# Attention into a soft mixture of experts: value tiles in one 128-row transfer, keys asked for earlier, key maxima and side work moved

## The chip, the cores and the metric

The kernel runs on one core of a Trainium2 chip. The metric is the device time of one execution in microseconds. Five engines matter, each with its own queue of instructions that it works off in order: PE (TensorE, matmuls and transposes; its weight loads are shown apart as PEld), DVE (VectorE), ACT (ScalarE), POOL (GpSimd) and SP (SyncE), which here only issues transfers from main memory. Semaphores order them between engines.

## The reference, cut to what matters

```python
# attention: q, k, v are (4 batches, 8 heads, 768 positions, 64), float32
k_sum = k.reshape(B, H, 24, 32, D).max(axis=3)      # one key per block of 32: the maximum
v_sum = v.reshape(B, H, 24, 32, D).mean(axis=3)     # and one value: the mean
scores_l = scale * q @ k.T, masked to |i - j| < 16  # the window
scores_s = scale * q @ k_sum.T + log(32)            # the 24 block keys
a = softmax(concat([scores_l, scores_s]))
x = a @ concat([v, v_sum])                          # -> (3072 tokens, 512)

# soft mixture of experts on x
logits = x @ phi                                    # (3072, 32 slots)
d = softmax of logits over the tokens;  slot_input = d.T @ x
slot_out[e] = relu(slot_input[e] @ w1[e]) @ w2[e]   # 8 experts, 4 slots each
c = softmax of logits over the slots;   return c @ slot_out
```

All of it is float32.

## The kernel before, in words

**Attention in 24 steps.** A step is 256 query positions of four heads. Three steps belong to one half of a batch's heads (`hb`, eight of them), which share one key tile; the table `STEPS` says which step is which, and `FIRST` = steps 0, 3, 6, 9, 12, 15, 18, 20 are those in which a new key tile is used for the first time. I call the step before each of these a boundary step (2, 5, 8, 11, 14, 17, 19).

In step `i` PE computes the scores of step `i` (`scores`, L210, into a PSUM tile `s` of which there is one), transposes the probabilities of step `j = i - 1` (`trans`, L253), and multiplies them with the values of step `j` (`values`, L268). DVE takes masked scores out of PSUM with their row minimum (`soft_max`, L231) and divides the previous step's output (`norm`, L283 to L285). ACT takes the exponentials (L240, L248) and moves the transposes out of PSUM (`evac`, L259). POOL subtracts the row values for the second half (`shift`, L244).

**Block keys.** The key tile holds, for each window of 64 keys, 24 columns kept free for the block maxima. `k_max` (L149, L158, L159, on DVE) reduces the tile, once for each of its two halves, and `k_put` (L164, POOL) copies the 24 maxima into each of the 12 windows, four windows first and then eight. `scores` of a `FIRST` step cannot start before its `k_put`.

**Block values.** A value tile `v` has 120 rows in use: 64 of the values, then 24 for block means, then 32 of the values. `v_sum` ("V" in the plans, L173) sums the values of three steps on PE; it needs all three value tiles of its half. `v_sel` ("S", L187) picks the 24 means, ACT copies them to `vsst`, and `put_v` (L196, POOL) copies them into rows 64 to 87 of each value tile.

**Side work.** The tables `PLAN_A` and `PLAN_B` place pieces of the second part between the steps: A between the transposes and `values`, B after `values`. X (or x) transposes 128 tokens of the attention's output and copies them out, on ACT for X and on DVE for x; L forms the logits of 512 tokens and, when the generator is run on, their maximum and exponentials; T transposes these, D multiplies them with the tokens and adds to `acc`. What a step started and did not finish stands in `pending` and is finished at the start of the next step.

**Transfers.** All are issued from SP, in the order of the program, at the end of each step: a key tile three steps before its use (`load_k`, two buffers), a query tile every other step (`load_q`, two buffers), the values of step `i + 5` (`load_v`, six buffers) and, by the table `LOADS`, pieces of expert weights of 512 KB (`load_piece`). The first 25 pieces have buffers of their own; the later ones take over buffers that attention has finished with. A transfer whose buffer is still in use holds up SP, and with it all that is behind it. `load_v` issues two transfers, one for 64 rows and one for 32.

**After attention** the rest of the routing follows, then a stream through the first expert matrices (L604), the second (L639) and the combination (L673), with the remaining weights loaded as buffers come free.

Of the kernel before, what the change touches and what calls it, by code (L numbers as in the profile page):

```python
# [18 lines left out]
NB = S // 32  # L19
HB = 2 * B  # L20
TPS = 3
NSTEP = HB * TPS
NQ = NT // 512
NW = S // 64

WA, WB = 64, 32
U = WA + NB + WB
SEG = WA + NB
KROW = SEG * (NW - 1) + U
VROW = 1152  # L30
NEG = -1.0e30
EPS = 1e-9

# [8 lines left out]
FIRST = [STEPS.index((hb, 0)) for hb in range(HB)]  # L42
STEP_OF = {s: i for i, s in enumerate(STEPS)}


LOADS = [0, 0, 1, 1, 1, 2, 1, 2, 1, 2, 1, 2, 1, 2, 1, 2, 1, 2, 2, 1, 1, 3, 2, 3]
NWA, NV, NX, NXT = 25, 6, 5, 4
LATE = "v v v k k v q p v q v p k r x x".split()


PLAN_A = {
    0: "V0", 3: "V1", 5: "X0", 6: "V2", 7: "X3", 8: "T0 X4", 9: "V3", 10: "X5", 11: "X6", 12: "V4", 13: "X8", 14: "X10",
    15: "V5", 16: "L2", 17: "X12", 18: "V6", 19: "X14", 20: "V7", 21: "X16", 22: "X18", 23: "L4", 24: "X20 T4",
}
PLAN_B = {
    0: "S0", 3: "S1", 5: "x1", 6: "S2 x2", 7: "L0", 9: "S3 D0", 11: "x7", 12: "S4 L1", 13: "x9 T1", 14: "D1",
    15: "S5 x11", 17: "x13 T2", 18: "S6 D2", 19: "x15", 20: "S7 L3", 21: "x17 T3", 22: "x19 D3", 24: "X21 D4",
}


# [1 line left out]
def attention_soft_moe(ctx: ExitStack, tc, kx, qx, vx, phi, wx, cst, out):  # L62

    nc = tc.nc
# [27 lines left out]
    wt = {}  # L92
# [25 lines left out]
    def load_k(hb, parts=1):  # L118
        if hb < HB:
            kt[hb] = kp.tile([128, 2, KROW], F32, name=f"k{hb}", tag="k")  # L120
            if parts == 1:
                nc.sync.dma_start(out=kt[hb].rearrange("p q k -> p (q k)"), in_=kx[hb].rearrange("p q k -> p (q k)"))
            else:
                for pr in range(2):
                    nc.sync.dma_start(out=kt[hb][:, pr], in_=kx[hb, :, pr])

    def load_q(n):
        if 2 * n < NSTEP:
            q = mx.tile([128, 2, 2, 256], F32, name=f"q{n}", tag="q")
            nc.sync.dma_start(out=q.rearrange("p i q t -> p (i q t)"), in_=qx[n])  # L130
            qt[2 * n], qt[2 * n + 1] = q[:, 0], q[:, 1]

    def load_v(i):
        if i < NSTEP:
            v = vp.tile([128, VROW], F32, name=f"v{i}", tag="v")
            nc.sync.dma_start(out=v[0:WA], in_=vx[i, 0:WA])
            nc.sync.dma_start(out=v[WA + NB : U], in_=vx[i, WA:])
            vt[i] = v[0:U, 0 : 16 * 65].rearrange("p (w h c) -> p w h c", w=4, h=4)


# [2 lines left out]
    def k_max(hb, pr):  # L143
        if pr == 0:
            ks[hb] = (
                wk.tile([128, 2, 4 * NW + 1], F32, name="k16", bufs=1), wk.tile([128, 2, NB], F32, name="ks", bufs=1)
            )
        k16, kb = ks[hb]
        nc.vector.reduce_max(  # L149
            out=k16[:, pr, 0 : 4 * NW].rearrange("p (w j) -> p w j", w=NW),  # L150
            in_=kt[hb][:, pr, 0 : SEG * NW].rearrange("p (w k) -> p w k", w=NW)[:, :, 0:WA].rearrange(
                "p w (j k) -> p w j k", j=4
            ),
            axis=AX,
        )
        if pr == 1:

            nc.vector.tensor_copy(out=k16[:, :, 4 * NW : 4 * NW + 1], in_=k16[:, :, 0:1])  # L158
            nc.vector.tensor_tensor(out=kb, in0=k16[:, :, 1 : 4 * NW : 2], in1=k16[:, :, 2 : 4 * NW + 1 : 2], op=ALU.max)  # L159

    def k_put(hb, eng, part=slice(0, NW)):
        dst = kt[hb][:, :, 0 : SEG * NW].rearrange("p q (w k) -> p q w k", w=NW)[:, :, part, WA:SEG]
        n = part.stop - part.start
        eng.tensor_copy(out=dst, in_=ks[hb][1].unsqueeze(2).broadcast_to([128, 2, n, NB]))  # L164
# [29 lines left out]
    def put_v(i, eng):  # L194
        src = vsst[STEPS[i][0] % 2][64 : 64 + NB].rearrange("n h c -> n (h c)").unsqueeze(1).broadcast_to([NB, 4, 260])
        eng.tensor_copy(out=vt[i][WA : WA + NB].rearrange("n w h c -> n w (h c)"), in_=src)  # L196
# [45 lines left out]
    def shift(i, r):  # L242
        p = p_[i][:, :, r]
        nc.gpsimd.tensor_tensor(out=p, in0=p, in1=m_[i, r].unsqueeze(2).broadcast_to([128, 4, U]), op=ALU.subtract)  # L244
# [11 lines left out]
    def evac(j, r):  # L256
        if r == 0:
            ptr_[j] = mx.tile([128, 2, 4, 128], F32, name="ptr", tag="r", bufs=1)
        nc.scalar.copy(out=ptr_[j][0:U, r], in_=ptr_[j, r])  # L259
# [188 lines left out]
    def flush(g):  # L448
        while advance(g):
            pass  # L450
# [9 lines left out]
    for i in range(TPS):  # L460
        load_v(i)
# [17 lines left out]
    def start(names):  # L479
        made = []  # L480
        for n in names.split():
            k, a = n[0], int(n[1:])
            if k in one_phase:
                one_phase[k](a)
            else:
                g = phased[k](a)
                advance(g)
                made.append(g)
                if k in "XxT":
                    flush(g)  # L490
                    made.pop()
        return made


    pending = []
    for i in range(NSTEP + 1):
        j = i - 1
        if i < NSTEP:
            scores(i)
        for g in pending:  # L500
            flush(g)
        if j in FIRST:
            put_v(j, nc.gpsimd)
        if j >= 0:
            trans(j, 0)
            trans(j, 1)
            evac(j, 0)
            evac(j, 1)
        if i < NSTEP:
            soft_max(i, 0)  # L510
            exp_units(i, 0)
            soft_max(i, 1)
            shift(i, 1)
            if i not in FIRST:
                put_v(i, nc.gpsimd)
        pending = start(PLAN_A.get(i, ""))
        if i < NSTEP:
            exp_wide(i, 1)
        if j >= 0:
            values(j, 0)  # L520
            values(j, 1)
        pending += start(PLAN_B.get(i, ""))
        if i + 1 in FIRST:
            hb = FIRST.index(i + 1)
            k_max(hb, 1)
            k_put(hb, nc.gpsimd, slice(0, 4))
            k_put(hb, nc.gpsimd, slice(4, NW))
        if j >= 0:
            norm(j)
        if i + 2 in FIRST:  # L530
            k_max(FIRST.index(i + 2), 0)
        if i < NSTEP:
            if i + 3 in FIRST[2:]:
                load_k(FIRST.index(i + 3))
            if i % 2:
                load_q((i + 3) // 2)
            load_v(i + 5)
            for _ in range(LOADS[i]):
                load_piece()

    tail.append(1)
# [58 lines left out]
    for k in range(32):  # L600
        e, c = divmod(k, 4)
# [21 lines left out]
    for i in range(2):  # L623
        nc.vector.tensor_copy(  # L624
            out=W2ST[i].rearrange("p j (e k) -> p j e k", e=NE)[:, :, :, 0:4],
            in_=ph[:, 128 * i : 128 * i + 128].rearrange("p (j e k) -> p j e k", j=4, e=NE),
# [85 lines left out]
def _layout(q, k, v, w1, w2):  # L712
    heads = np.arange(8).reshape(2, 2, 2)
    t = np.arange(NW)[:, None] * 64 - 16 + np.arange(64)[None, :]
    kx = np.zeros((HB, 128, 2, KROW), np.float32)
    qx = np.zeros((NSTEP // 2, 128, 2, 2, 256), np.float32)
    vx = np.ones((NSTEP, WA + WB, VROW), np.float32)
    for hb in range(HB):
        b, half = divmod(hb, 2)
        for pr in range(2):  # L720
            for r in range(2):
                h = heads[half, pr, r]
                kt = k[b, h].T
                rows = kx[hb, 64 * r : 64 * r + 64, pr]
                for w in range(NW):
                    rows[:, SEG * w : SEG * w + WA] = kt[:, t[w] % S]
                rows[:, SEG * NW :] = kt[:, np.arange(752, 784) % S]
                for tp in range(TPS):
                    n, i = divmod(STEP_OF[hb, tp], 2)
                    qx[n, 64 * r : 64 * r + 64, i, pr] = q[b, h, 256 * tp : 256 * tp + 256].T  # L730
        for w in range(NW):
            i, wi = STEP_OF[hb, w // 4], w % 4
            rows = (64 * w - 16 + np.arange(WA + WB)) % S

            for n in range(4):
                c = 65 * (4 * wi + n)
                vx[i, :, c : c + 64] = v[b, 4 * half + n, rows]
    wx = np.zeros((NPIECE, 128, 1024), np.float32)
    wx[0:32] = w1.reshape(NE * 4, 128, DF)
    n = 32  # L740

    wr = w2.reshape(NE, 4, 2, 128, DM)
    for c0, cn in CHUNKS:
        part = wr[..., c0 : c0 + cn].transpose(0, 2, 3, 1, 4)
        if cn == 128:
            part = part.transpose(0, 2, 1, 3, 4)
        part = part.reshape(-1, 128, 1024)
        wx[n : n + len(part)] = part
        n += len(part)
    return kx, qx.reshape(NSTEP // 2, 128, 1024), vx, wx  # L750
# [46 lines left out]
```

## Time and profile before

| what | value |
|---|---|
| three runs | 230.48, 233.22, 235.27 us; median 233.22 |
| the profiled execution | 228.62 us, of which the span of instructions is 226.7 |
| PE busy | 188.0 us, 83% |
| DVE, ACT, POOL busy | 125.6, 99.9, 58.4 us |
| moved by transfers | 66.54 MB, 293 GB/s on average |
| the queue that SP issues to | 90.5% of 16 transfer engines |

The span falls into a start until about 16 us, the steps 1 to 23 until about 158 us, the rest of the routing until about 171 us, and the expert stages. The table's shares are means over these. "PE busy" says nothing of the clock that PE ran at, which the profile lists apart.

### The profile page before, as it was taken

To read this page: it belongs to the slowest core of one execution; us is meant where nothing else is said; L and a number is where in the kernel's file an instruction comes from. 1 tells how busy PE (TensorE), PEld (TensorE's weight loads), DVE (VectorE), ACT (ScalarE), POOL (GpSimd) and SP (SyncE) were. 2 spreads that over 40 slices of the span, in tenths; PEclk is the share of its full clock that TensorE was granted. 3 is DMA by queue.
4 is the path that set the end of the run, shared out by engine and by line. 5 is a ranking of instruction groups with operands and counts; after the bars stand their busy time and mean duration, and the time that the engine had idled before them with its cause. 6 is when DMAs were issued, how large, how long until landed. Compare 5 with 4: busy or idle time off the path is not lost.

```text
span 226.7 us, 7484 instructions
## 1 busy us (share of the span) xinstructions
PE 188.0 (83%) x3021; PEld 132.0 (58%) x3021; DVE 125.6 (55%) x610; ACT 99.9 (44%) x254; POOL 58.4 (26%) x74
## 2 busy tenths in 40 slices
PE   7469499599699499969957959999879999999970
PEld 6227378467568368745845647767544555564740
DVE  2506758638858635880776664676544575035361
ACT  2225468166568254734572545755520232025251
POOL 2215533433433411351432241445001000000000
PEclk9958999799999758985996988999985999999985
DMA  6999999999999999999999890388795999999666
GB/s 238 288 337 247 261 372 246 280 365 302 290 331 271 280 277 336 262 267 329 267 301 325 255 346 12 116 298 273 257 387 178 307 418 405 408 407 380 264 277 277
DMA packets 17746, 66.54 MB, mean 293 GB/s; under 512 B 2864, under 2 KB 2864, under 8 KB 16816
## 3 DMA queue, kind: packets, MB, share of 16 engines
q1 hardware_dynamic: 17712, 66.07, 90.5%
q8 instruction: 24, 0.39, 0.8%
q14 instruction: 10, 0.08, 0.1%
HBM read 59.77 MB, written 6.29 MB: 291 GB/s over the span
## 4 chain that ended last, share of the span: by engine, by line
PE 69%; DVE 12%; ACT 5%; DMA 4%; issue 4%; POOL 2%; SPq 2%; ACTq 0%; POOLq 0%; DVEq 0%
PE s L210 11%; PE pt L253 10%; PE o L268 9%; PE hps L604 7%; PE so L639 7%; PE pp L173 6%; DMA v<-vx 4%; PE op L673 4%; PE pp L307 3%; DVE k L149 3%; PE pp L323 2%; PE pp L366 2%; DVE p L231 2%; PE pp L187 2%; DVE xt L311 2%
## 5 line engine op out<-in xcount | busy, mean ns | idle before, releaser
L231 DVE CUSTOM_DVE_ANT_0 p<-s,cs 128x120 f32<-128x120 f32 x192 | 40.7, 278 | 19.3 <-PE s L210 19.3
L259 ACT COPY ptr<-pt 120x512 f32<-120x512 f32 x48 | 26.3, 589 | 45.0 <-PE pt L253 44.8
L210 PE MATMUL s<-k,q 64*64 64x120 f32 x768 | 29.1, 296 | 18.9 <-POOL k L164 17.5
L244 POOL TENSOR_TENSOR p<-p,m 128x480 f32<-128x480 f32 x24 | 23.7, 988 | 66.3 <-DVE m L231 41.9
L210 PEld LDWEIGHTS s<-k,q 64*64 64x64 f32 x768 | 22.9, 149 | 26.5 <-POOL k L164 19.6
L240 ACT ACTIVATE p<-p,m 128x120 f32<-128x120 f32 x96 | 30.1, 392 | 7.2 <-DVE m L231 7.2
L196 POOL COPY v<-vsst 24x1040 f32<-24x1040 f32 x24 | 25.2, 1051 | 26.0 <-ACT vsst L190 13.8
L268 PEld LDWEIGHTS o<-v,ptr 120*64 120x64 f32 x768 | 26.1, 145 | 9.4 <-issue 5.7
L268 PE MATMUL o<-v,ptr 120*64 120x65 f32 x768 | 29.4, 232 | 2.6 <-issue 2.6
L253 PE MATMUL pt<-ident,p 128*120 128x128 f32 x192 | 30.3, 307 | 0.2 <-ACT p L248 0.2
L253 PEld LDWEIGHTS pt<-ident,p 128*120 128x120 f32 x192 | 23.8, 153 | 4.9 <-issue 4.1
L173 PE MATMUL pp<-v,cs 64*32 64x256 f32 x192 | 16.0, 466 | 3.1 <-DMA v<-vx 3.1
L285 DVE TENSOR_TENSOR x<-o,z 128x512 f32<-128x512 f32 x24 | 16.6, 691 | 1.7 <-PE pp L366 0.9
L149 DVE TENSOR_REDUCE k<-k 128x48 f32<-128x768 f32 x16 | 15.1, 945 | 3.7 <-DMA k<-kx 3.7
L248 ACT ACTIVATE p<-p 128x480 f32<-128x480 f32 x24 | 14.5, 606 | 5.3 <-POOL p L244 5.3
L604 PE MATMUL hps<-w,W1ST 128*32 128x256 f32 x240 | 16.2, 412 | 0.1
L231 DVE DVE_READ_ACCUMULATOR2_ANT m<- 128x1 f32 x192 | 15.9, 83 | 0.0
L311 DVE COPY xt<-pp 128x512 f32<-128x512 f32 x10 | 6.9, 692 | 15.5 <-PE pp L307 15.5
L307 PE MATMUL pp<-ident,x 128*128 128x128 f32 x92 | 14.4, 279 | 0.0
L283 DVE TENSOR_SCALAR z<-o 128x8 f32<-128x8 f32 x24 | 3.9, 162 | 18.5 <-PE o L268 18.5
L674 DVE COPY ot<-op 128x512 f32<-128x512 f32 x12 | 8.2, 690 | 7.6 <-PE op L673 7.6
L639 PE MATMUL so<-w,W1ST 128*32 128x128 f32 (+1 forms) x192 | 11.5, 312 | 0.4 <-DVE W1ST L624 0.4
(114 smaller groups left out, 209.8 us busy)
## 6 DMA issues: line engine op xcount, KB each, us to landing
w<-wx SPq DMA_DIRECT2D x61, 512.0 KB, 8.0
k<-kx SPq DMA_DIRECT2D x7, 1088.0 KB, 8.9
v<-vx SPq DMA_DIRECT2D x24, 288.0 KB, 7.7
q<-qx SPq DMA_DIRECT2D x12, 512.0 KB, 9.0
out<-ot SPq DMA_DIRECT2D x12, 512.0 KB, 3.9
v<-vx SPq DMA_DIRECT2D x24, 144.0 KB, 7.7
k<-kx SPq DMA_DIRECT2D x2, 544.0 KB, 4.4
wk<-wx SPq DMA_DIRECT2D x2, 512.0 KB, 6.7
```

Of the source, the lines that this page charges most:

```text
L149: nc.vector.reduce_max(out=k16[:, pr, 0 : 4 * NW].rearrange("p (w j) -> p w j", w=NW), in_=kt[hb][:, pr, 0 : SEG * NW].rearrange("p (w k) ...
L173: nc.tensor.matmul(pv[32 * g : 32 * g + 32, 0:256], lhsT=cs[0:WA, c : c + 32], rhs=v[0:WA, g, :, 0:64], start=(tp == 0), stop=(tp == TPS - 1),
L196: eng.tensor_copy(out=vt[i][WA : WA + NB].rearrange("n w h c -> n w (h c)"), in_=src)
L210: nc.tensor.matmul(s[64 * ab : 64 * ab + 64, r, U * u : U * u + U], lhsT=qt[i][64 * r : 64 * r + 64, pr, c : c + 64], rhs=kt[hb][64 * r : ...
L231: nc.vector.tensor_tensor_reduce(out=p_[i][:, u, r], in0=sv[:, u, :], in1=maskv[:, mk, :], scale=-0.125, scalar=-NEG, op0=ALU.add, op1=ALU ...
L240: nc.scalar.activation(out=p[:, u, r], in_=p[:, u, r], func=AF.Exp, scale=-1.0, bias=m[:, u : u + 1])
L244: nc.gpsimd.tensor_tensor(out=p, in0=p, in1=m_[i, r].unsqueeze(2).broadcast_to([128, 4, U]), op=ALU.subtract)
L253: nc.tensor.transpose(pt[:, u, :], p_[j][:, u, r], ident)
L259: nc.scalar.copy(out=ptr_[j][0:U, r], in_=ptr_[j, r])
L268: nc.tensor.matmul(o_[j][64 * ab : 64 * ab + 64, tt, 2 * pr + r], lhsT=ptr[0:U, r, u, 64 * ab : 64 * ab + 64], rhs=v[:, 2 * tt + ab, 2 * p ...
L604: nc.tensor.matmul(hps[32 * j : 32 * j + 32, :], lhsT=W1ST[:, c, 32 * e : 32 * e + 32], rhs=t[:, j, :], start=(k == 0), stop=(k == 31), ti ...
L639: nc.tensor.matmul(so[32 * j : 32 * j + 32, :], lhsT=W2ST[i][:, j, 32 * e : 32 * e + 32], rhs=t[:, j, :], start=(e == 0 and i == 0), stop= ...
```

## The change

- A value tile comes in one transfer to all 128 partitions, 1088 columns wide (before, 96 rows of 1152 columns in two transfers). The rows for block means and the eight unused rows are carried along as ones. That is 544 KB a step instead of 432 KB.
- `load_k` is issued four steps before the use, for the third to the seventh key tile (at steps 2, 5, 8, 11, 14); the last, whose first use comes after two steps and not three, at step 17 as before.
- The weight pieces that have buffers of their own are issued ahead of the step's values, not behind.
- In a boundary step `k_max` of the second half and `k_put` stand right behind `soft_max`, and the first four windows are put ahead of `put_v` on POOL. `k_max` of the first half, one step earlier, stands there too.
- What is pending from the step before (logit maxima, `acc`) is finished behind these and no longer ahead of the transposes and of `soft_max`.
- The plans: V moves from the `FIRST` step, where it stood between transposes and `values`, to the end of the boundary step before; S moves from the end of the `FIRST` step to its middle; all the ten x on DVE become X on ACT, some in other steps; T0 to T4 move by a slot or two.

```diff
-VROW = 1152
+VROW = 1088
-LOADS = [0, 0, 1, 1, 1, 2, 1, ...
+LOADS = [0, 1, 1, 1, 1, 2, 1, ...
 PLAN_A = {
-    0: "V0", 3: "V1", 5: "X0", 6: "V2", 7: "X3", 8: "T0 X4", 9: "V3", ...
+    0: "V0", 3: "S1", 5: "X0", 6: "S2 X1", 7: "X3", 8: "X4", 9: "S3 T0", ...
 PLAN_B = {
-    0: "S0", 3: "S1", 5: "x1", 6: "S2 x2", 7: "L0", 9: "S3 D0", ...
+    0: "S0", 2: "V1", 5: "V2", 6: "X2", 7: "L0", 8: "V3", 9: "D0", 11: "V4", ...
     def load_v(i):
             v = vp.tile([128, VROW], F32, name=f"v{i}", tag="v")
-            nc.sync.dma_start(out=v[0:WA], in_=vx[i, 0:WA])
-            nc.sync.dma_start(out=v[WA + NB : U], in_=vx[i, WA:])
+            nc.sync.dma_start(out=v, in_=vx[i])
...
             scores(i)
-        for g in pending:
-            flush(g)
         if j in FIRST:
             put_v(j, nc.gpsimd)
...
             shift(i, 1)
+            if nxt is not None:          # i + 1 is a FIRST step
+                k_max(nxt, 1)
+                k_put(nxt, nc.gpsimd, slice(0, 4))
             if i not in FIRST:
                 put_v(i, nc.gpsimd)
+            if nxt is not None:
+                k_put(nxt, nc.gpsimd, slice(4, NW))
+            if nxt2 is not None:         # i + 2 is a FIRST step
+                k_max(nxt2, 0)
+        for g in pending:
+            flush(g)
         pending = start(PLAN_A.get(i, ""))
...
-        if i + 1 in FIRST:
-            hb = FIRST.index(i + 1)
-            k_max(hb, 1)
-            k_put(hb, nc.gpsimd, slice(0, 4))
-            k_put(hb, nc.gpsimd, slice(4, NW))
         if j >= 0:
             norm(j)
-        if i + 2 in FIRST:
-            k_max(FIRST.index(i + 2), 0)
         if i < NSTEP:
-            if i + 3 in FIRST[2:]:
-                load_k(FIRST.index(i + 3))
+            hb = FIRST.index(i + 4) if i + 4 in FIRST[2:7] else 7 if i == 17 else HB
+            load_k(hb)
             if i % 2:
                 load_q((i + 3) // 2)
+            for n in range(LOADS[i]):
+                if len(wt) < NWA:
+                    load_piece()
             load_v(i + 5)
-            for _ in range(LOADS[i]):
+            while len(wt) < sum(LOADS[: i + 1]):
                 load_piece()
```

DVE in the boundary step 5, before: the last rows of `soft_max` of step 5 (L231), then a copy of side work (L311), the key maxima for step 6 (L149 to L159) and `norm` (L283 to L285).

```order
L231 ISA p,m<-s,cs 128x120
L231 ISA m 128x1
L311 COPY xt<-pp 128x512
L149 TENSOR_REDUCE k_535<-k_456 128x48
L158 COPY k_535<-k_535 128x2
L159 TENSOR_TENSOR ks<-k_535 128x48
L283 TENSOR_SCALAR z<-o 128x8
```

The same place in the changed kernel:

```order
L231 ISA p,m<-s,cs 128x120
L231 ISA m 128x1
L149 TENSOR_REDUCE k_506<-k_374 128x48
L158 COPY k_506<-k_506 128x2
L159 TENSOR_TENSOR ks<-k_506 128x48
L283 TENSOR_SCALAR z<-o 128x8
```

The copy of x1, which needs a PE transpose that comes after `values`, no longer stands between `soft_max` and the key maxima.

PE from the scores of boundary step 5 to the transposes of step 6, before (`k_145` is the key tile of steps 3 to 5, `k_456` that of steps 6 to 8, the `v` of L173 are the value tiles of steps 6 to 8):

```order
L210 MATMUL s<-k_145,q_284 64x120 x16
L253 MATMUL pt<-ident,p 120x128 x8
L307 MATMUL pp<-ident,x_276 128x128 x4
L268 MATMUL o<-v_152,ptr 64x65 x16
L307 MATMUL pp<-ident,x_276 128x128 x4
L210 MATMUL s<-k_456,q_458 64x120 x16
L253 MATMUL pt<-ident,p 120x128 x8
L173 MATMUL pp<-v_286,cs 32x256 x4
L173 MATMUL pp<-v_364,cs 32x256 x4
L173 MATMUL pp<-v_460,cs 32x256 x4
```

And in the changed kernel:

```order
L210 MATMUL s<-k_142,q_278 64x120 x16
L253 MATMUL pt<-ident,p 120x128 x8
L307 MATMUL pp<-ident,x_273 128x128 x4
L268 MATMUL o<-v_148,ptr 64x65 x16
L173 MATMUL pp<-v_282,cs 32x256 x4
L173 MATMUL pp<-v_378,cs 32x256 x4
L173 MATMUL pp<-v_456,cs 32x256 x4
L210 MATMUL s<-k_374,q_452 64x120 x16
L253 MATMUL pt<-ident,p 120x128 x8
```

The twelve sums of V2 now stand ahead of the first scores on the new keys, in place of the transposes of x1.

## Rows read from the trace of the kernel before

**Rows 1.** The page: span, and the transfer engines' busy tenths in 40 slices.

```profile
span 226.7 us, 7484 instructions
...
DMA  6999999999999999999999890388795999999666
```

**Rows 2.** Windows: stretch, its length, busy us of each engine, PE clock, transfer share, GB/s.

```profile
16.20:158.00 141.80, 120.03 (x2125) 92.10 (x2125) 90.06 (x494) 77.43 (x202) 53.64 (x62) 0.90 0.94 277
...
77.50:86.00 8.50, 8.49 (x100) 5.98 (x104) 2.27 (x18) 3.21 (x8) 1.39 (x2) 0.50 1.03 303
...
134.80:158.00 23.20, 22.41 (x413) 17.75 (x414) 14.51 (x86) 13.55 (x36) 8.75 (x10) 0.93 0.55 182
...
34.20:36.20 2.00, 1.66 (x51) 1.51 (x52) 1.30 (x12) 1.98 (x6) 0.85 (x1) 1.00 1.06 218
...
180.00:205.00 25.00, 24.62 (x413) 14.70 (x405) 10.59 (x38) 5.34 (x12) 0.00 (x0) 1.00 1.01 405
```

**Rows 3.** The page's transfers: tile, issuer, count, KB each, median us from issue to landing.

```profile
w<-wx SPq DMA_DIRECT2D x61, 512.0 KB, 8.0
k<-kx SPq DMA_DIRECT2D x7, 1088.0 KB, 8.9
v<-vx SPq DMA_DIRECT2D x24, 288.0 KB, 7.7
q<-qx SPq DMA_DIRECT2D x12, 512.0 KB, 9.0
...
v<-vx SPq DMA_DIRECT2D x24, 144.0 KB, 7.7
```

**Rows 4.** Chain of waits, start: issues of the first key tile's two halves (start, us).

```profile
0.73 0.39 SPq L125
1.18 0.42 SPq L125
```

**Rows 5.** Tile k, stretch 0.7 to 1.6 us: issue to landing of these two.

```profile
DMA to landing us min/median/max: 3.9/4.4/4.8
```

**Rows 6.** Timeline of SP: last issues for the values of steps 1, 2 and 23.

```profile
4.33 0.59 SPq L137 DMA_DIRECT2D v<-vx  x1
...
6.00 0.31 SPq L137 DMA_DIRECT2D v<-vx  x1
...
127.30 0.58 SPq L137 DMA_DIRECT2D v<-vx  x1
```

**Rows 7.** Tile v, three stretches (from 3.8, 4.96, 126.5 us): issue to landing.

```profile
DMA to landing us min/median/max: 8.0/8.1/8.1
...
DMA to landing us min/median/max: 8.2/8.4/8.6
...
DMA to landing us min/median/max: 4.5/4.6/4.7
```

**Rows 8.** Waits: who for whom, us in total, times, longest.

```profile
PEld s L210 <- POOL k L164: 19.6, 7, 3.2
...
PEld pp L173 <- DMA v<-vx: 3.8, 5, 1.6
```

**Rows 9.** Timeline, boundary step 11 into 12 (start, us, instruction, idle before).

```profile
74.02 0.08 DVE L231 DVE_READ_ACCUMULATOR2_ANT m<- 128x1 f32 x1
...
75.23 0.94 DVE L149 TENSOR_REDUCE k<-k 128x48 f32<-128x768 f32 x1
...
77.12 0.79 POOL L164 COPY k<-ks 128x192 f32<-128x192 f32 x2 [0.39 <-POOL v L196]
...
77.51 1.88 PE L210 MATMUL s<-k,q 64*64 64x120 f32 x32 [2.93 <-POOL k L164]
```

**Rows 10.** Timeline of PE: the last third of V0, and step 1's scores.

```profile
13.63 1.08 PE L173 MATMUL pp<-v,cs 64*32 64x256 f32 x8 [0.65 <-DMA v<-vx]
...
16.19 1.88 PE L210 MATMUL s<-k,q 64*64 64x120 f32 x32
```

**Rows 11.** Groups by line: side work's copies on ACT (busy us, mean ns).

```profile
L313 ACT COPY xt<-pp 128x512 f32<-128x512 f32 x13 | 7.6, 581 | 0.9 <-PE pp L307 0.9
```

More of the change, by code (lines that the diff above doesn't have):

```diff
@@ L43 @@
 STEP_OF = {s: i for i, s in enumerate(STEPS)}
-LOADS = [0, 0, 1, 1, 1, 2, 1, 2, 1, 2, 1, 2, 1, 2, 1, 2, 1, 2, 2, 1, 1, 3, 2, 3]
+LOADS = [0, 1, 1, 1, 1, 2, 1, 2, 1, 2, 1, 2, 1, 2, 1, 2, 1, 1, 2, 1, 1, 3, 2, 3]
 NWA, NV, NX, NXT = 25, 6, 5, 4
@@ L51 @@
 PLAN_A = {
-    0: "V0", 3: "V1", 5: "X0", 6: "V2", 7: "X3", 8: "T0 X4", 9: "V3", 10: "X5", 11: "X6", 12: "V4", 13: "X8", 14: "X10",
-    15: "V5", 16: "L2", 17: "X12", 18: "V6", 19: "X14", 20: "V7", 21: "X16", 22: "X18", 23: "L4", 24: "X20 T4",
+    0: "V0", 3: "S1", 5: "X0", 6: "S2 X1", 7: "X3", 8: "X4", 9: "S3 T0", 10: "X5", 11: "X6", 12: "S4 X7", 13: "X8",
+    14: "T1 X10", 15: "S5", 16: "L2", 17: "X12", 18: "S6 T2", 19: "X14", 20: "S7", 21: "X16", 22: "X18 T3", 23: "L4",
+    24: "X20 X21",
 }
 PLAN_B = {
-    0: "S0", 3: "S1", 5: "x1", 6: "S2 x2", 7: "L0", 9: "S3 D0", 11: "x7", 12: "S4 L1", 13: "x9 T1", 14: "D1",
-    15: "S5 x11", 17: "x13 T2", 18: "S6 D2", 19: "x15", 20: "S7 L3", 21: "x17 T3", 22: "x19 D3", 24: "X21 D4",
+    0: "S0", 2: "V1", 5: "V2", 6: "X2", 7: "L0", 8: "V3", 9: "D0", 11: "V4", 12: "L1", 13: "X9", 14: "V5 D1", 15: "X11",
+    17: "V6 X13", 18: "D2", 19: "V7 X15", 20: "L3", 21: "X17", 22: "X19 D3", 24: "T4 D4",
 }
@@ L508, in attention_soft_moe @@
             evac(j, 1)
+        nxt = FIRST.index(i + 1) if i + 1 in FIRST else None
+        nxt2 = FIRST.index(i + 2) if i + 2 in FIRST else None
         if i < NSTEP:
@@ L716, in _layout @@
     qx = np.zeros((NSTEP // 2, 128, 2, 2, 256), np.float32)
-    vx = np.ones((NSTEP, WA + WB, VROW), np.float32)
+    vx = np.ones((NSTEP, 128, VROW), np.float32)
     for hb in range(HB):
@@ L733, in _layout @@
             rows = (64 * w - 16 + np.arange(WA + WB)) % S
+            place = np.r_[0:WA, WA + NB : U]
             for n in range(4):
                 c = 65 * (4 * wi + n)
-                vx[i, :, c : c + 64] = v[b, 4 * half + n, rows]
+                vx[i, place, c : c + 64] = v[b, 4 * half + n, rows]
     wx = np.zeros((NPIECE, 128, 1024), np.float32)
```

## The prediction

> **What bounds the kernel now.** I read the page first. Its row of transfer busy tenths [rows 1] stands at 9 from the second slice to the twenty-third, that is to about 130 us: the transfer engines never run dry in attention. Next the windows [rows 2]: in attention PE is busy 120.0 of 141.8 us, at 0.90 of its clock. So two resources are nearly full there, transfers and PE, and the question is which of the two is slow for a reason that the change takes away. I think both are.
>
> *Transfers.* From 180 to 205 us, when only weights come in, they move 405 GB/s at a share of 1.01 [rows 2]; from 34.2 to 36.2 us, among value loads, 218 GB/s at 1.06 [rows 2]. The engines are as busy and move half. What a value load costs shows at the start, where everything queues. The values of step 1 have landed at 4.33 + 8.1 = 12.4 us, those of step 2 at 6.00 + 8.2 = 14.2 us [rows 6, 7]: 1.8 us for 432 KB, some 245 GB/s. The two halves of the first key tile, each 544 KB on 128 partitions, land at 0.73 + 3.9 = 4.63 and 1.18 + 4.8 = 5.98 us [rows 4, 5]: 1.35 us, or 413 GB/s. The changed value load has exactly this form, 128 x 1088.
>
> *PE.* In seven boundary steps PE stands 19.6 us in all before scores that wait for `k_put` [rows 8]. In the chain of step 11 into 12 [rows 9], `soft_max` ends at 74.10, but the key maxima start only at 75.23 (DVE waits for a PE transpose that it copies first), POOL puts `put_v` ahead of `k_put`, and PE goes on at 77.51. The wait then costs more: from 77.5 to 86.0 us PE is busy without a break at a clock of 0.50 [rows 2], the lower of its two levels, 1.2 GHz, after 2.93 us of standing still [rows 9]. Over attention the clock of 0.90 [rows 2] means that up to 0.10 x 141.8 = 14 us went that way.
>
> **The value load.** Bytes first. Until the last values (step 23) there are in the changed kernel 8 x 1088 KB of keys, 24 x 544 of values, 11 x 512 of queries and 25 x 512 of weights: 40,192 KB, 41.2 MB. Before it was 24 x 432 of values and 23 x 512 of weights: 36,480 KB, 37.4 MB, landed at 127.30 + 4.7 = 132.0 us [rows 3, 6, 7]. Less some 3 us until the first bytes run that is 290 GB/s. At 405 GB/s the 41.2 MB take 101.7 us, so the last values can have landed at 104.7 us, 27 us earlier, though they are more bytes. Ends for the unseen rate of the mixture: 290 GB/s (nothing gained) and 413. I take 405, since its form is that of the key halves and the rest are full transfers like the weights.
>
> The Trainium skill, DMA: Bandwidth & Descriptors, section Rules for kernel authors, says that two transfers to disjoint partition halves share the same 16 engines and serialize, and that one 128-partition transfer is to be used. Taken as a rule on bytes alone it speaks against this change, since it would price the old pair at 432 KB of full rate and the new load at 544 KB. The landings above disagree with that price: 1.8 us for the smaller pair, 1.35 us for the larger transfer.
>
> **The start.** V0's last third starts at 13.63 when the values of step 2 arrive, and step 1's scores at 16.19 [rows 10]. Ahead of those values lie constants and three value loads; with 1.35 for 1.8 us each they arrive some 1.4 us earlier. Step 1 starts at 14.8.
>
> **PE's own work.** At full clock attention needs between 120.0 - 14 = 106 us and 120 us of PE [rows 2]; the row of clock 0.50 with PE busy in full says that most of the lost clock fell on busy time, so I take 108. The plans move the sums and transposes and add none.
>
> **The boundaries.** In the new order, after `soft_max` ends there remain the maxima (0.94), two short DVE instructions (0.8 together as they stood, from 76.17 to 77.0) and the first `k_put` (0.4): 2.1 us [rows 9]. Beside them V, moved here, gives PE work in place of the wait: 12 sums, 1.1 us for four at the low clock at the start [rows 10], so 1.6 at full clock. I leave 0.7 us idle at each of seven boundaries, 5 us for 19.6, and no fall of the clock. POOL: `put_v` now waits behind `k_put`, but its reader, the next step's `values`, comes more than 2 us later. Late next is V itself, which needs a value load half a step to a step sooner (a rival below).
>
> **Edits at nothing.** Ten copies go from DVE to ACT, 10 x 0.58 = 5.8 us [rows 11]; ACT is busy 77.4 of 141.8 us [rows 2] and would have 83 of some 115. Without that slack they would cost up to 5.8 us. Logit maxima finished later delay T only, a step on. Keys asked for a step earlier: 1.1 MB takes 2.7 us at 405 GB/s, and there are two steps for it; without that, DVE would stand at `k_max`. Weights ahead of values on SP have free buffers and hold up nothing; they put values 512 KB or 1.3 us back, once or twice a step, and their reader comes two steps later.
>
> **The sum.** PE alone: 14.8 + 108 = 122.8 for what was reached at 158. From step 20 to there PE has 22.4 us of work at 0.93 of the clock, 20.8 at full [rows 2]; some 20 once V7 lies ahead of it. So PE reaches the end of V7 at 102.8, with the idle bits at 108; transfers allow it from about 105. Two limits as close as this wait for each other now here, now there; I add 4 us (chosen; between 0 and the 5 us of the boundaries again). V7 ends at 112, attention's mark at 132 instead of 158. The rest, 68.7 us [rows 1, 2], is untouched: its own weights wait for buffers that the first expert stage frees. 132 + 68.7 = 200.7 us of span, and 1.9 us around it: **202.6** against 228.62 for the profiled execution. That execution is below all three timed runs, whose median of 233.22 is 1.020 times as long; on their scale the forecast is **207 us**.
>
> **The rivals.**
> - *A. The mixture reaches less than 405 GB/s.* For it: no row shows values of the new form among keys and queries in attention. At 350 GB/s the last values land at 120.7; attention's mark is at 121 + 20 = 141, 17 us early: 211.6, on the runs' scale 216. The page on DMA, section Specifications, gives a limit of about 358 GB/s per core from main memory; by it the values would land at 118, the mark would be at 138 and the median at 213. The trace does not agree: 405 GB/s over 25 us.
> - *B. V waits where the keys waited.* V stands ahead of the scores, and values sometimes arrived late for it already, 3.8 us in five waits [rows 8]. If a value load lands 2.5 us late at each boundary, the idle time is 19.6 us again and the clock falls as before: 26 us come back, no change (229 to 233). It decides if the landing takes longer than some two steps, 9 us; before, the medians were 7.7 us [rows 3]. Against it: less queue ahead at a faster rate.
> - *C. Slower: the low rate is not the form's doing.* Then 41.2 MB at 290 GB/s take 142 us, values land at 145, 13 us later than before, and every earlier gain on PE only waits: mark at 145 + 20 = 165, 7 us late, 236 on the profile's scale, 240 on the runs'. The point from which it decides: below about 305 GB/s over attention the mark is past 158. Against it speaks the 413 GB/s of the key halves.
> - *D. PE alone sets the pace:* no mutual waiting, no idle bits, mark at 123: 193.5, or 197.
>
> **How the numbers follow.** The forecast has 0.60, A 0.16, B 0.09, C 0.06, D 0.09. The range reaches from D to a bit beyond A, 197 to 222; B and C stay outside. A change of about 2% is the least that a measurement of this kernel can tell. Faster by more: the forecast, A, D and a bit of B, 0.87. Within: most of B, 0.07. Slower: C, 0.06.
>
> **What would show it.** GB/s in attention's slices at 370 or more; values landing 4 to 7 us after issue; waits of scores for `k_put` under 8 us; a PE clock of 0.95 or more in attention; the expert stages as long as before. I am wrong if the rate stays near 290, if L173 waits for values by over 10 us, or if the time after attention grows by what attention loses.

## The result, and the profile after

The changed kernel takes 208.21 us (median of four, 207.57 to 209.44) against 234.25 (230.48 to 235.76): a ratio of 0.899, interval 0.887 to 0.910. Some executions of a kernel fall into a slower state at a lower granted clock, which the ratios and the times of the experiments leave out: here 235.27 and 235.76 of the kernel before, so that 0.899 is 208.36 to 231.85 and not the ratio of the medians. The forecast was 207, in a range of 197 to 222. Its profiled execution took 209.44 us, the longest of its four.

The page of the changed kernel: span, granted PE clock, busy tenths of the transfer engines and GB/s in 40 slices of 5.2 us.

```profile
span 207.7 us, 7466 instructions
...
PEclk9979999999799999999999999999959999999985
DMA  5999999999998999999999336878949999989466
GB/s 219 416 405 406 418 400 414 406 411 408 377 376 291 310 401 339 370 364 337 315 395 346 138 104 195 294 245 297 389 122 336 419 406 410 406 343 403 191 281 243
```

The transfer engines are as busy as in [rows 1], but from the second slice on they move some 410 GB/s where some 290 were moved before. From about the eleventh slice the figure falls below 380. In part they have less work there: from 60 to 65 us their share is 0.89, at 336 GB/s. In part they are slower while busy: from 90 to 95 us they move 298 GB/s at a share of 1.00, and why is not shown.

Windows of the changed kernel, with the columns of [rows 2]: attention, two stretches of it, and the rest.

```profile
16.20:138.00 121.80, 109.02 (x2098) 83.38 (x2094) 84.96 (x485) 82.65 (x212) 53.15 (x61) 0.98 0.91 336
20.00:50.00 30.00, 27.86 (x544) 21.53 (x543) 22.18 (x138) 21.09 (x53) 14.24 (x17) 1.00 1.02 409
20.00:100.00 80.00, 72.56 (x1400) 55.69 (x1401) 56.04 (x331) 53.86 (x137) 35.09 (x41) 0.98 0.99 374
138.00:207.70 69.70, 57.90 (x825) 33.97 (x823) 30.58 (x95) 18.28 (x44) 1.70 (x2) 0.90 0.84 325
```

Attention's mark, the last transposes of its probabilities, stood at 158 us and stands at 138; the rest is 69.7 us for 68.7. PE is busy 109.0 us of 121.8 instead of 120.0 of 141.8 [rows 2], with the same work, since its clock is 0.98 for 0.90.

Waits in the changed kernel (who for whom, us in total, times, longest):

```profile
PEld pp L307 <- ACT lt L345: 4.3, 3, 1.6
PEld s L210 <- POOL k L164: 2.5, 4, 0.9
PEld pp L173 <- DMA v<-vx: 2.4, 2, 1.3
PEld pp L173 <- ACT lt L345: 2.2, 1, 2.2
...
PEld pp L173 <- ACT lt L339: 1.4, 1, 1.4
```

The wait for `k_put`, 19.6 us in [rows 8], is 2.5 us. In its place stand three rows that end in `lt`, 7.9 us together, 6.8 of them before attention's mark, none of which the forecast had. V waits for values only 2.4 us, all of it before step 1. The timeline of boundary step 8 shows where they come from (start, us, instruction, idle before):

```profile
50.13 0.95 DVE L149 TENSOR_REDUCE k<-k 128x48 f32<-128x768 f32 x1
...
51.56 0.28 DVE L337 TENSOR_REDUCE stat<-pp 128x1 f32<-128x128 f32 x1
...
51.88 0.37 ACT L338 ACTIVATE dt<-pp,stat 128x128 f32<-128x128 f32 x1 [0.66 <-DVE stat L337]
...
52.23 0.26 ACT L339 COPY lt<-pp 128x128 f32<-128x128 f32 x1
...
52.54 1.50 PE L173 MATMUL pp<-v,cs 64*32 64x256 f32 x24 [1.26 <-ACT lt L339]
...
53.97 1.84 PE L210 MATMUL s<-k,q 64*64 64x120 f32 x32
```

L0's logits lie in one of the two PSUM banks `pp` until their maximum, their exponentials and their copy `lt` are done. The change does these behind the key maxima. V3 needs the bank, PE stands 1.26 us, the scores of step 9 come late behind V3, and they run at the low clock (1.84 us for the 1.05 of a step at full clock; the granted clock from 53.97 to 55.81 us is 0.53).

Boundary step 11, for comparison with [rows 9]: `soft_max` ends at 67.52, the maxima follow at once, V4 runs beside them, and the scores follow V4 with a wait of 0.40 us.

```profile
67.44 0.08 DVE L231 DVE_READ_ACCUMULATOR2_ANT m<- 128x1 f32 x1
67.44 0.95 DVE L149 TENSOR_REDUCE k<-k 128x48 f32<-128x768 f32 x1
67.52 1.50 PE L173 MATMUL pp<-v,cs 64*32 64x256 f32 x24
...
69.02 0.34 POOL L164 COPY k<-ks 128x192 f32<-128x192 f32 x1 [0.33 <-DVE ks L159]
...
69.42 0.85 PE L210 MATMUL s<-k,q 64*64 64x120 f32 x24 [0.40 <-POOL k L164]
```

### The profile page after: what moved, and what is told of

Its sections match the earlier page's. It is cut to its first block, busy times and chain, and to the rows that moved or that the text cites. A ratio compares the mean times of both kernels' runs of the same rounds, so it can differ in the third digit from the quotient of the medians.

```text
span 207.7 us, 7466 instructions
## 1 busy us (share of the span) xinstructions
PE 178.3 (86%) x3021; PEld 124.6 (60%) x3021; DVE 120.3 (58%) x601; ACT 104.7 (50%) x263; POOL 58.7 (28%) x74
## 4 chain that ended last, share of the span: by engine, by line
PE 69%; DVE 9%; ACT 9%; DMA 6%; issue 3%; SPq 1%; POOL 1%; ACTq 0%; DVEq 0%; POOLq 0%
PE s L210 11%; PE pt L253 9%; PE hps L610 8%; PE o L268 8%; PE so L645 7%; DMA v<-vx 6%; PE pp L173 5%; PE op L679 3%; PE pp L307 3%; DVE p L231 3%; PE pp L366 3%; ACT ptr L259 3%; PE pp L323 2%; PE pp L187 2%; ACT p L240 2%
## 5 line engine op out<-in xcount | busy, mean ns | idle before, releaser
L231 DVE CUSTOM_DVE_ANT_0 p<-s,cs 128x120 f32<-128x120 f32 x192 | 40.8, 279 | 25.9 <-PE s L210 25.9
L268 PE MATMUL o<-v,ptr 120*64 120x65 f32 x768 | 27.9, 225 | 2.5 <-issue 2.1
L268 PEld LDWEIGHTS o<-v,ptr 120*64 120x64 f32 x768 | 24.5, 137 | 7.5 <-issue 6.8
L210 PE MATMUL s<-k,q 64*64 64x120 f32 x768 | 26.8, 280 | 1.0 <-DVE k L164 0.6
L253 PE MATMUL pt<-ident,p 128*120 128x128 f32 x192 | 27.3, 286 | 0.0
L210 PEld LDWEIGHTS s<-k,q 64*64 64x64 f32 x768 | 21.1, 139 | 9.2 <-issue 4.8
L253 PEld LDWEIGHTS pt<-ident,p 128*120 128x120 f32 x192 | 21.2, 141 | 4.3 <-issue 3.8
L173 PE MATMUL pp<-v,cs 64*32 64x256 f32 x192 | 12.8, 381 | 8.0 <-DMA v<-vx 2.3
L285 DVE TENSOR_TENSOR x<-o,z 128x512 f32<-128x512 f32 x24 | 16.6, 691 | 4.8 <-PE pp L366 4.1
L149 DVE TENSOR_REDUCE k<-k 128x48 f32<-128x768 f32 x16 | 15.2, 950 | 3.6 <-DMA k<-kx 3.6
L231 DVE DVE_READ_ACCUMULATOR2_ANT m<- 128x1 f32 x192 | 16.0, 83 | 0.0
L307 PEld LDWEIGHTS pp<-ident,x 128*128 128x128 f32 x92 | 10.3, 141 | 6.4 <-ACT lt L345 4.3
L313 ACT COPY xt<-pp 128x512 f32<-128x512 f32 x22 | 12.8, 584 | 0.7 <-PE pp L307 0.6
L173 PEld LDWEIGHTS pp<-v,cs 64*32 64x32 f32 x192 | 5.1, 106 | 12.8 <-DMA v<-vx 2.4
```

Source lines behind the costliest of these rows:

```text
L173: nc.tensor.matmul(pv[32 * g : 32 * g + 32, 0:256], lhsT=cs[0:WA, c : c + 32], rhs=v[0:WA, g, :, 0:64], start=(tp == 0), stop=(tp == TPS - 1),
L210: nc.tensor.matmul(s[64 * ab : 64 * ab + 64, r, U * u : U * u + U], lhsT=qt[i][64 * r : 64 * r + 64, pr, c : c + 64], rhs=kt[hb][64 * r : ...
L231: nc.vector.tensor_tensor_reduce(out=p_[i][:, u, r], in0=sv[:, u, :], in1=maskv[:, mk, :], scale=-0.125, scalar=-NEG, op0=ALU.add, op1=ALU ...
L253: nc.tensor.transpose(pt[:, u, :], p_[j][:, u, r], ident)
L268: nc.tensor.matmul(o_[j][64 * ab : 64 * ab + 64, tt, 2 * pr + r], lhsT=ptr[0:U, r, u, 64 * ab : 64 * ab + 64], rhs=v[:, 2 * tt + ab, 2 * p ...
L285: nc.vector.tensor_tensor(out=xh[n][:, :, 256 * half : 256 * half + 256].rearrange("p t (k d) -> p t k d", k=4), in0=o_[j][:, :, :, 0:64], ...
```

## The experiments

Theory F says that the form of the value load sets the rate of all transfers and that this bound attention; rival S that the order of work made the gain. Ratios below are against the kernel before, run on the same chip beside each. The changed kernel itself did not run beside the experiments, and on one of their three chips the kernel before was faster (228.92 and 230.41 us in its two shortest runs), so that a difference of 2 us from the changed kernel's 208.2 tells little.

**The old value loads in the changed kernel.** With `VROW` 1152 again; all other edits stay.

```diff
-            nc.sync.dma_start(out=v, in_=vx[i])
+            nc.sync.dma_start(out=v[0:WA], in_=vx[i, 0:WA])
+            nc.sync.dma_start(out=v[WA + NB : U], in_=vx[i, WA:])
```

> The changed kernel with the old value loads alone (two transfers, 64 and 32 rows of 1152 columns). Theory F, the form of the value load sets the rate at which everything arrives: GB/s in attention fall back to about 290, the last values land near 132 us again and the time goes back to 225 to 234 us, the new order of work notwithstanding. Rival S, the order on DVE, POOL and PE made the gain and transfers were hidden: the time stays within 3% of the changed kernel's 208, at most 214 us.

232.4 us, ratio 0.997 (0.992 to 1.003): all of the gain is gone, as F says. The rate from 20 to 100 us, and the waits (the edit shifts line numbers by one, as some edits below do):

```profile
20.00:100.00 80.00, 66.36 (x1190) 49.73 (x1189) 48.05 (x276) 47.47 (x123) 30.86 (x37) 0.91 1.03 292
```

```profile
PEld pp L174 <- DMA v<-vx: 17.2, 5, 8.5
...
PEld s L211 <- POOL k L165: 1.7, 3, 0.8
```

The waits at `k_put` are gone here too (1.7 us), but PE stands 17.2 us before V, which waits for values. The better order alone only reaches the transfers' limit sooner. This is rival B of the prediction, at the old rate.

**The new value load in the kernel before.** The same edit the other way round, with `VROW` 1088.

> The kernel before with the new value load alone (one transfer to 128 rows, 1088 columns); order and plans are the old ones. Theory F: GB/s go to 350 or more while there is work queued, the waits of PE and DVE for transfers (some 10 us in all) go, but the seven waits of scores for k_put stay near 19 us with their falls of the clock, so about half of the gain: 218 to 226 us. Rival S: nothing waited for transfers long enough, 230 to 236 us.

224.9 us (223.9 to 227.1), ratio 0.967 (0.958 to 0.976), in the upper part of what F gave. The waits of scores are untouched, and the transfers are no longer full:

```profile
PEld s L209 <- POOL k L163: 19.2, 7, 3.1
```

```profile
20.00:100.00 80.00, 66.19 (x1178) 50.80 (x1181) 53.56 (x295) 44.36 (x115) 30.65 (x37) 0.91 0.89 320
```

The first of these two refutes S as the whole story, the second F: alone, all other edits give 0.3%, which the interval does not tell from nothing, and the load 3.3%, a third of the gain where F expected half; together they give 10.1%. Each takes away one of two limits that stood close together.

**Rows, pieces or bytes.** The same 544 KB a step, in two transfers of 64 rows each, and in two of 128 rows and half of the columns each.

```diff
-            nc.sync.dma_start(out=v, in_=vx[i])
+            nc.sync.dma_start(out=v[0:64], in_=vx[i, 0:64])          # two halves
+            nc.sync.dma_start(out=v[64:128], in_=vx[i, 64:128])
...
+            nc.sync.dma_start(out=v[:, 0:544], in_=vx[i, :, 0:544])  # two columns
+            nc.sync.dma_start(out=v[:, 544:1088], in_=vx[i, :, 544:1088])
```

> The changed kernel with each value tile in two transfers of 64 rows, one after the other, with the same 128 rows and the same bytes. If it is the rows that one transfer covers that slow it (theory F), a pair costs at least the 1.8 us of the old one and the time is 225 us or more. If it is only the sum of the bytes that counts, the two share the engines and come out as one: 208 us, at most 211.

> The changed kernel with each value tile in two transfers, each to all 128 rows and half of the columns (272 KB each, the same size and number as two halves of 64 rows in e3, which gave 252.8 us). If the rows that one transfer covers set the rate: 207 to 211 us. If the number of transfers or their smaller size does: 225 or more.

Two halves of rows: 247.6 us, a single run; its profiled execution took 254.96. Two halves of columns: 207.68 us, ratio 0.894 (0.889 to 0.898), the same as one transfer. Two windows each, at the start where almost only values come in, and in attention; first the halves of rows, then the halves of columns:

```profile
9.10:16.10 7.00, 2.78 (x24) 0.58 (x24) 1.71 (x16) 1.25 (x4) 0.99 (x1) 0.65 1.05 251
20.00:100.00 80.00, 62.52 (x1014) 45.10 (x1012) 41.57 (x245) 40.65 (x103) 27.15 (x32) 0.84 1.03 280
```

```profile
8.00:12.30 4.30, 3.75 (x47) 1.14 (x36) 1.71 (x16) 1.25 (x4) 0.99 (x1) 1.00 1.09 389
20.00:100.00 80.00, 72.02 (x1420) 55.05 (x1416) 57.97 (x335) 55.05 (x142) 36.72 (x44) 1.00 1.01 386
```

The number of transfers and their size are the same. The rows that one transfer covers make 251 GB/s of 389 and 40 us of the kernel's time. The halves of rows have rows twice as long as the halves of columns, but that is not it: the single transfer has the same long rows and goes at 409 GB/s. Why a transfer to fewer rows is slower is not shown.

**The places of the key maxima and of the side work.** Old places of `k_max` and `k_put`; old plan tables; both.

```diff
             shift(i, 1)
-            if nxt is not None:
-                k_max(nxt, 1)
-                k_put(nxt, nc.gpsimd, slice(0, 4))
...
         pending += start(PLAN_B.get(i, ""))
+        if nxt is not None:
+            k_max(nxt, 1)
+            k_put(nxt, nc.gpsimd, slice(0, 4))
+            k_put(nxt, nc.gpsimd, slice(4, NW))
...
```

> The changed kernel with key maxima and k_put alone back at the end of the step, behind the plan B work on DVE and behind put_v on POOL. Rival S says that this place made the gain: seven waits of about 2.5 us return with falls of the clock, 220 to 232 us. Theory F: copies on DVE and x are gone from between, V covers a part, so 1 to 2 us at each of seven boundaries: 211 to 222 us.

> The changed kernel with the two old plan tables alone: V back in the first step on the new keys, S at its end, ten copies on DVE. Theory F: the boundaries lose the cover of V (1.4 us each of seven) and put_v comes later, 5 to 15 us slower, 213 to 223. Rival S: the order around the keys would be undone with it, 225 or more. If the timetable is worth nothing, 207 to 210.

> The changed kernel with both the old place of key maxima and k_put and the old plans; the new value loads, order of transfers and late finish stay. Each alone cost about 2 us. If they are separate terms, 212 to 214 us. If each covers for the other (V under the wait for the keys, early keys where V is missing), the seven waits of 2 to 3 us and the falls of the clock come back only here: 217 to 224 us.

Old maxima: 210.18 us, ratio 0.904 (0.897 to 0.910), not told from the changed kernel's 0.899. Old plans: 210.58 us, on the faster chip; against the two runs before named above that is 0.918, so they may be worth 2 to 4 us, which is not settled. Both lie below the ranges that F gave. Both together: 234.3 and 235.4 us, ratio 1.010 (1.005 to 1.016), far beyond the upper end of 224 us that I gave. The waits of scores for `k_put` in the three, in this order, and the window of the third:

```profile
PEld s L210 <- POOL k L164: 7.8, 6, 2.1
```

```profile
PEld s L209 <- POOL k L163: 5.7, 5, 1.7
```

```profile
PEld s L209 <- POOL k L163: 17.9, 6, 3.5
```

```profile
16.20:157.00 140.80, 116.06 (x1966) 89.01 (x1965) 86.39 (x468) 73.16 (x191) 48.35 (x56) 0.85 0.77 278
```

With either of them in its new place the waits stay at 6 to 8 us in pieces of at most 2.1 us, and the clock holds (0.96 from 16.2 to 138 us in both). With both gone, six waits of about 3 us come back and the clock falls to 0.85. V under the wait and early maxima are two covers of one hole. That the sum is even worse than the new load with the whole old order (0.967) fits the late finish of pending work, which is still in it: PE waits 7.9 us in attention there for `lt` and for `dt`, the tile of the exponentials. It was not tried apart.

**The order of transfers.** Keys three steps ahead again, weights behind the values.

> The changed kernel with the old order of transfers alone: keys three steps ahead and weight pieces behind the values. With the new form at about 400 GB/s a key tile takes 2.7 us and lands before its maxima are due: 207 to 211, not told from the changed kernel. If asking early was needed, DVE waits for keys 2 to 3 us at each of five boundaries: 215 to 222.

210.69 us (210.29 to 212.63), within the 207 to 211 that I gave for no need to ask early. The trace says that there is some need. DVE's waits for keys, here and in the changed kernel:

```profile
DVE k L149 <- DMA k<-kx: 8.1, 5, 3.2
```

```profile
DVE k L149 <- DMA k<-kx: 3.6, 2, 3.2
```

Three waits are added, 1.5 us each. The time is 2.5 us above the changed kernel's, and 0.920 against the two runs before on that chip, which would make it nearly 5: asking earlier is worth 2 to 5 us, not settled closer.

**When pending work is finished.** Back at the start of the step, and between `soft_max` and the key maxima.

```diff
             scores(i)
+        for g in pending:           # at the start of the step
+            flush(g)
...
             shift(i, 1)
+        for g in pending:           # or here, behind soft_max
+            flush(g)
...
-        for g in pending:
-            flush(g)
         pending = start(PLAN_A.get(i, ""))
```

> The changed kernel with what is pending finished at the start of the step again, ahead of the transposes' copies and soft_max. In the changed kernel PE waits some 6 us in all for the copy of the logits (lt) that frees one of two PSUM banks: the later finish made a new wait. If that wait is what holds it, this gains 3 to 6 us (202 to 206). If the early finish holds up soft_max and the evacuation as much, it is the same or up to 4 us slower (208 to 212).

> The changed kernel with what is pending finished right behind soft_max, ahead of the key maxima. The PSUM bank comes free 1 to 1.5 us sooner in four steps and nothing ahead of soft_max is held up; the maxima start up to 0.7 us later, which V covers. If the wait for the bank costs what the trace shows: 3 to 5 us faster (203 to 206). If not: 207 to 209.

At the start: 202.59 us (201.73 to 203.66), 5.6 us below the changed kernel, but on the faster chip. Against the two runs before there it is 0.882, which makes the gain about 4 us; the two kernels that differ from the changed one by old plans or old transfers alone took 210.6 and 210.7 on the same chip. Behind `soft_max`: 205.5 us (203.94 to 206.84), a smaller gain, and not told apart; in its profiled execution, of 210.79 us, 5.6 of the 6.8 us of waits for `lt` in attention are still there. With the finish at the start one is left, the transfers are full, and attention's mark lies at 132.5 us:

```profile
PEld pp L307 <- ACT lt L345: 0.9, 1, 0.9
```

```profile
20.00:100.00 80.00, 75.88 (x1509) 57.86 (x1506) 59.49 (x341) 58.21 (x150) 37.76 (x45) 1.00 1.01 393
```

**A version that beats both.** Early finish, five weight pieces moved behind the last values, and then value rows without their 48 unused columns.

```diff
-LOADS = [..., 2, 1, 2, 1, 2, 1, 2, 1, 1, 2, 1, 1, 3, 2, 3]
+LOADS = [..., 2, 1, 1, 1, 1, 1, 1, 1, 0, 1, 5, 2, 3, 2, 3]
...
...
-VROW = 1088
+VROW = 1040                 # the second of the two alone
```

> The changed kernel with what is pending finished at the start of the step (as in e5, 202.6 us) and five weight pieces moved from steps 11 to 18 to steps 19 to 22, behind the last values. If transfers are the limit that is left, the last values land up to 6 us sooner, V7 no longer waits and the fall of the clock at step 20 goes: 198 to 201 us. If PE's own work is the limit: 202 to 203.

> As e10, with value rows of 1040 columns, the ones in use, for 1088: 0.6 MB less to move, 1.4 us at 405 GB/s. If transfers still bind: up to 1.5 us below e10. If not: the same as e10 within 1 us.

201.37 us, ratio 0.866 (0.863 to 0.870), and 199.8 us, ratio 0.859 (0.856 to 0.863). Both lie below the changed kernel's interval of 0.887 to 0.910, and below the 0.894 of the halves of columns, which ran on the same chip. What the moved pieces add to the early finish is 1 us by the times and nearly 4 by the ratios on two chips, and 201.37 lies between what I gave for either limit. The narrower rows give about 1.5 us more, as they would if transfers still bound it. Neither was settled. With the narrower rows PE is busy 106.9 of 112.4 us of attention, at full clock:

```profile
16.20:128.60 112.40, 106.93 (x2091) 81.69 (x2090) 83.31 (x484) 81.76 (x210) 52.83 (x61) 1.00 0.95 358
```

## Why the prediction was right, and where it was not

- **Two limits, both released: right.** That the transfers bound attention through the form of the value load, and PE through the seven boundaries, is shown by the two single changes, 0.997 and 0.967, against 0.899 for both. Rival C (the rate is not the form's doing) is refuted by the 409 GB/s and by the halves of rows and of columns, rival B (V waits in place of the keys) by V's 2.4 us of waits for values here, rival D (PE alone, mark at 123) by the mark at 138. One reading was off, and nothing hangs on it: the row of tenths in [rows 1] stands at 9 to the twenty-second slice, not the twenty-third.
- **The rate: mechanism right, size too high.** I took 405 GB/s until the last values and let them land at 104.7 us. The rate holds while the engines are full (409 from 20 to 50 us) but is 374 over 20 to 100 us. The last values are issued only at 108.80 and land 6.0 us later, at 114.8. The median from issue to landing is 7.5 us, beyond the 4 to 7 that I gave as a sign:

```profile
108.80 0.33 SPq L137 DMA_DIRECT2D v<-vx  x1
```

```profile
DMA to landing us min/median/max: 6.0/6.0/6.0
```

```profile
v<-vx SPq DMA_DIRECT2D x24, 544.0 KB, 7.5
```

  The count of bytes lacked a term: SP issues a value load only when PE has finished with its buffer, and waits for that as it did before (60.3 us there).

```profile
SPq L137 <- PE o L268: 44.2, 18, 6.0
```

  With the early finish the last values are issued at 102.90 and land at 110.0, and the rate over 20 to 100 us is 393 GB/s: a part of what the rate lacked was PE's delay. Rival A (less than 405) came true in part. The 41.2 MB until 114.8 us are some 368 GB/s, reckoned as in the prediction, and the mark lies near the 141 us that A had for 350, but the early finish alone moves it to 132.5.

- **PE's own work: right.** 109.0 us at a clock of 0.98 is 107 at full clock, for the 108 that I took.
- **The boundaries: right, slightly too dear.** 2.5 us of waits for the 5 that I left, and step 1 starts at 14.4 for 14.8. Behind step 1, whose scores ran at the low clock again (1.88 us), the clock fell once all the same in attention, at step 9, behind the wait for `lt`.
- **"Edits at nothing": this step failed.** "Logit maxima finished later delay T only" overlooked that the same instructions free the PSUM bank that V and X need next. It made 6.8 us of new waits in attention, of which taking it back left 0.9, and that gave 4 to 6 us.
- **The page on two transfers to disjoint halves** (the Trainium skill, DMA: Bandwidth & Descriptors, Rules for kernel authors): its advice to use one 128-partition transfer held here, with 232.4 us for two, of 64 and 32 rows, and 208.2 for one. Read as a price by bytes alone it failed: the same bytes a step took 247.6 us in two halves of rows.
- **The sum.** V7 ended at 116.1 for 112 and attention's mark came at 138 for 132; with the early finish it is 132.5, so the late finish is most of that. The rest took 1 us more. On the scale of profiled executions that is 209.4 against my 202.6, 6.8 us off. That the median came within 1.2 us owes something to luck: I scaled by 1.020 because the profiled execution before was faster than the timed ones, while the one after is slower than the rest. Between the medians the change is 26.0 us, what the sum gave; by the runs that the ratio uses it is 23.5, and between the profiled executions 19.2.

## What to carry to other kernels

A transfer engine's busy share said nothing of its speed here (1.03 at 292 GB/s, 1.02 at 409): compare the GB/s of a mixed stretch with a pure one, and when they differ at the same share, look at the form of the transfers; here it was one that covers part of the rows. When two limits stand close together, test each edit both ways, alone and taken away, since neither of two covers of one hole shows a price while the other stands. Moving the end of a piece of work costs what waits for its buffer, not only what waits for its result.

## What the runs showed of the hardware

Two transfers of 64 rows each move 251 GB/s at the start of the kernel, where two of the same size and 128 rows move 389 GB/s. In attention the other transfers seem to suffer with them: 280 GB/s in all at a busy share of 1.03, though the values are less than a third of the bytes. A third at 251 GB/s and the rest at the 405 of [rows 2] would make some 340 (an estimate). The kernel is 40 us longer. I had expected 225 us or more from the halves of rows, and not 247.6, 15 more than with the old pair of 64 and 32 rows, which moved fewer bytes.
